# A gated attention and MLP decode step: the order of the first loads, and keys transposed ahead of the query

## The chip, the cores and the metric

The kernel runs on one core of one Trainium2 chip. The metric is the device time of one execution in microseconds (us); less is better. Each time is told as the median of the runs shown. One further execution was taken with the hardware profiler; its span, in the page, runs from the first to the last instruction of the program.

## The reference

Eight sequences each decode one token `x` of 448 numbers. Two branches are computed from it and mixed by a gate. All inputs are bf16.

```python
# A: attention over the last W = 1024 of 4096 cached positions, 16 query heads on 8 key heads, Dh = 256
q = (x @ wq).reshape(B, Sq, Hq, Dh).transpose(0, 2, 1, 3)           # wq: 448 x 4096
k = jnp.repeat(k_cache[:, :, Sk - W:, :], rep, axis=1)
v = jnp.repeat(v_cache[:, :, Sk - W:, :], rep, axis=1)
p = softmax(einsum("bhqd,bhkd->bhqk", q, k) * Dh ** -0.5)
a = einsum("bhqk,bhkd->bhqd", p, v).transpose(0, 2, 1, 3).reshape(B, Sq, Hq * Dh) @ wo
# B: layer norm and a two-layer MLP, 448 -> 1792 -> 448
b = gelu(layernorm(x) @ w1 + b1) @ w2 + b2
g = sigmoid((x * gate_w).sum(-1, keepdims=True))
out = g * a + (1 - g) * b
```

Nearly all bytes are the cache: per sequence 4 MB of keys and 4 MB of values, 64 MB in all; wq and wo are 3.5 MB each, w1 and w2 some 1.5 MB each.

## The kernel before, in words

**Loads.** A ring of four slots in SBUF, 32 KB per partition each, takes all large loads (`ring`, line 82). `add` (line 108) puts loads on a plan in the order in which they are to be used. `pump` (line 98) issues the next loads of the plan as long as no more than four slots are given out and not yet used up, and `done` (line 104) counts a slot as used up and pumps. All these loads are issued by SP, one after the other. A load into a slot that was in use waits, on SP, until the last readers of the slot are done, and whatever SP has to issue later waits behind it. The plan (lines 162 to 177) is: wq; the keys of batch 0 (k0), in two halves of 2 MB; then k1, v0, k2, v1 and so on to k7, v6; w1; v7 with w2; wo in eight pieces. `half_loader` (line 115) loads one batch in two halves by heads, `pair_loader` (line 125) in one piece, `rows_loader` (line 137) a list of matrices into one slot, one behind the other.

**wq.** Its 448 rows are 384 and 64. The first 384 lie three to a partition (`wq_m`, line 147) and are loaded as one block of 4096 columns (1 MB) and one of 8192 (2 MB). The last 64 rows are cut in half, so that they fill 128 partitions of 2048 columns (`wq_t`, line 148, 512 KB). Before, all three pieces stand in one slot, the half rows first, the others behind them from column `OWQ` on (line 156).

**The start.** `moments` (line 254) turns `x` so that it can be the stationary side of the query's matmuls (`turned`, line 227, into `xw`) and takes the mean and the variance for the layer norm; its last step is a square root on ACT. `query` (line 384) computes the query of all batches in 28 matmuls of width 512 on PE: 8 and 16 over wq's two blocks (line 390, `stationary`), 4 over the half rows (line 402, `ends`). Then ACT copies the result out (`qs`, line 412), DVE turns it (`qt`, line 415), and DVE and ACT lay it out as the stationary side of the scores (`qw`, line 428, eight copies each). `gate` (line 262) takes the gate's logits on DVE, a tanh on ACT, and a few small tables (`perm`, `pick`, `mask`); `gall` and `oall` hold the gate and its complement on all partitions.

**A batch.** `transpose_keys` (line 352) turns 1024 x 8 keys so that the head dimension lies on the partitions. The work is cut in 16 blocks, eight for each of two `kt` tiles. Block 0 (in batches 2, 4 and 6 blocks 0 and 1) is turned by DVE (line 339) and laid out by 16 copies on POOL (line 347). Each other block is four transposes on PE (line 371) into one of three PSUM tiles `ktp`, and one copy out of it on ACT (the blocks in `BY_ACT`, line 377) or DVE (line 379). Between the blocks the steps of the batch before are called, by a table from block number to steps (`between`; `steps`, line 599). `scores` (line 430) does 32 matmuls against `qw` into `S_ps`, `top` (line 447) takes the maximum. `expo`, `turn`, `scale` and `bring` make the softmax weights of the batch before, `values` (line 502) multiplies them with the values, `finish` and `spread` collect the results.

**The order of the program** is written out by hand in lines 617 to 638; each engine works through its own instructions in that order:

```python
    moments()
    query()
    gate()
    transpose_keys(0)
    scores(0)
    top(0)
    for b in range(1, NB):
        transpose_keys(b, steps(b - 1))
        scores(b)
        top(b)
        values(b - 1)
```

**The end.** After the last values the MLP's second layer and the output projection run as 46 chunks of matmuls while wo's pieces arrive, with a few filling matmuls between them (`run_on`, line 650); DVE adds two partial sums (line 690), and two stores write the result.

Of the kernel before, what the change touches and what calls it, by code (L numbers as in the profile page):

```python
# [11 lines left out]
BF16 = mybir.dt.bfloat16  # L12
# [5 lines left out]
def kernel(  # L18
# [15 lines left out]
    nc = tc.nc  # L34
    P = nc.NUM_PARTITIONS
# [3 lines left out]
    HD = A_wq.shape[1]  # L39
# [18 lines left out]
    QN = 512  # L58
# [22 lines left out]
    consts = ctx.enter_context(tc.tile_pool(name="consts", bufs=1))  # L81
# [16 lines left out]
    def pump():  # L98
        while len(slots) < min(len(plan), consumed[0] + RING):
            t = ring.tile([P, SLOT], BF16, tag="slot", name="slot")  # L100
            plan[len(slots)](t)
            slots.append(t)

    def done(n=1):
        consumed[0] += n
        pump()

    def add(key, loader):
        index[key] = len(plan)
        plan.append(loader)  # L110

    def slot(*key):
        return slots[index[key]]

    def half_loader(src, b):
        def load(t):
            for i in range(NG):
                v = src[b, i:Hkv:NG, kv_base:Sk, :].rearrange(
                    "a (s c) d -> s a (c d)", c=NCK
                )  # L120
                nc.sync.dma_start(t[:, i * HS : (i + 1) * HS], v)

        return load
# [13 lines left out]
    def rows_loader(pieces):  # L137
        def load(t):
            o = 0
            for ap in pieces:  # L140
                n = ap.shape[-1]
                nc.sync.dma_start(t[:, o : o + n], ap)
                o += n

        return load

    wq_m = A_wq[0:DM, :].rearrange("(p r) n -> p (r n)", r=NR)
    wq_t = A_wq[DM:D, :].rearrange("r (h n) -> (r h) n", h=2)
# [4 lines left out]
    OW1T = NR * F  # L153
    OW2 = OW1T + FH
    wq_r = [wq_m[:, 0:HD], wq_m[:, HD : NR * HD]]
    OWQ = HD // 2

    def last_values(t):
        pair_loader(A_v_cache, NB - 1, 2)(t)
        nc.sync.dma_start(slot("w12")[:, OW2 : OW2 + FB * D], w2_v)  # L160

    add(("wq",), rows_loader([wq_t] + wq_r))
    add(("k", 0), half_loader(A_k_cache, 0))
    for b in range(1, NB):
        add(("k", b), (half_loader if b == NB - 1 else pair_loader)(A_k_cache, b))
        add(("v", b - 1), pair_loader(A_v_cache, b - 1))
# [11 lines left out]

    x_sb = consts.tile([NB, D], BF16)
    consts.tile([P, SHIFT], F32, name="shift")  # L180
    pump()
    nc.scalar.dma_start(x_sb[:], xf)
    g_b = consts.tile([NB, D], BF16)
# [70 lines left out]
    def moments():  # L254
        turned(0, nc.vector.tensor_copy, nc.vector.tensor_copy)
        nc.vector.bn_stats(stats[:], x_sb[:])
        nc.vector.bn_aggr(mv[:], stats[:])
        nc.scalar.activation(
            rstd[:], mv[:, 1:2], ACT.Sqrt, bias=eps_t[:], scale=1.0
        )  # L260

    def gate():
        prod = consts.tile([NB, D], F32)
        gl = consts.tile([NB, 1], F32)
        nc.vector.scalar_tensor_tensor(
            prod[:],
            in0=x_sb[:],
            scalar=1.0,
            in1=g_b[:],
            op0=ALU.mult,  # L270
            op1=ALU.mult,
            accum_out=gl[:],
        )
        gth = consts.tile([NB, 1], F32)
        nc.scalar.activation(gth[:], gl[:], ACT.Tanh, scale=0.5)
        nc.vector.tensor_copy(
            perm[:].rearrange("p (s a) -> p s a", a=QD),
            ident[:].rearrange("p (a s) -> p s a", a=QD),
        )
        nc.vector.reduce_sum(  # L280
            pick[:],
            ident[:].rearrange("p (g b) -> p b g", g=QD)[:, 0:NB, :],
            axis=AXIS.X,
        )
        nc.vector.reduce_sum(
            mask[:],
            ident[:]
            .rearrange("p (s o a) -> p a o s", a=QD, o=1)
            .to_broadcast([P, QD, rep, SK]),
            axis=AXIS.X,  # L290
        )
        nc.vector.tensor_scalar(
            g32[0:NB, 0:1], gth[:], 0.5, 0.5, op0=ALU.mult, op1=ALU.add
        )
        nc.vector.tensor_scalar(om[:], gth[:], -0.5, 0.5, op0=ALU.mult, op1=ALU.add)
        gt = consts.tile([BL, BL], F32)
        nc.vector.transpose(gt[:], g32[:])
        gb = consts.tile([BL, BL], F32)
        nc.vector.stream_shuffle(gb[:], gt[:], [0] * BL)
        for i in range(QD):  # L300
            nc.scalar.copy(gall[BL * i : BL * (i + 1), :], gb[:, 0:NB])
        nc.vector.tensor_scalar(oall[:], gall[:], -1.0, 1.0, op0=ALU.mult, op1=ALU.add)
# [20 lines left out]
    def stationary(a, r):  # L323
        o = (a * NX + r) * GAP + BL
        return flat[:, o : o + NB]

    def ends(a, x2):
        o = (a * NX + NR) * GAP
        m = GAP + NB + BL * x2
        o += 0 if x2 else BL  # L330
        return flat[:, o : o + m], m
# [20 lines left out]
    def transpose_keys(b, between=None):  # L352
        between = between or {}
        kn = slot("k", b)[:].bitcast(F32)
        for hh in range(NG):
            kt = ktpool.tile([P, QD, NCK, SK, NJ], BF16, tag="kt", name="kt")
            KT[hh] = kt
            for i in range(NCK // CB):
                g = hh * (NCK // CB) + i
                n = 2 if b in DOUBLE else 1  # L360
                if g < n:
                    if g == 0:
                        turn_blocks(kn, kt, n * CB)
                    for step in between.get(g, ()):
                        step()
                    continue
                ktp = ps_kt.tile([P, CB, P, NJ], BF16, tag="ktp", name="ktp")
                words = ktp[:].bitcast(F32)
                for c in range(CB):
                    o = (hh * NCK + i * CB + c) * P  # L370
                    nc.tensor.transpose(  # L371
                        words[:, c, :, 0], kn[:, o : o + P], ident_f[:]
                    )
                dst = kt[:, :, i * CB : (i + 1) * CB, :, :]
                src = ktp[:].rearrange("p c (s a) t -> p a c s t", a=QD)
                if g in BY_ACT:
                    nc.scalar.copy(dst, src)  # L377
                else:
                    nc.vector.tensor_copy(dst, src)  # L379
                for step in between.get(g, ()):  # L380
                    step()
        done()

    def query():
        w = slot("wq")
        for r in range(NR):
            for n in range(W // QN):
                for t in range(QD):
                    o = OWQ + r * HD + t * W + n * QN
                    nc.tensor.matmul(  # L390
                        S_ps[BL * t : BL * t + NB, n * QN : (n + 1) * QN],
                        lhsT=stationary(0, r),
                        rhs=w[:, o : o + QN],
                        start=(r == 0),
                        stop=False,
                        skip_group_check=True,
                    )
        for n in range(W // QN):
            for x2 in range(2):
                lhsT, m = ends(0, x2)  # L400
                o = x2 * W + n * QN
                nc.tensor.matmul(  # L402
                    S_ps[0:m, n * QN : (n + 1) * QN],
                    lhsT=lhsT,
                    rhs=w[:, o : o + QN],
                    start=False,
                    stop=(x2 == 1),
                    skip_group_check=True,
                )
        done()  # L410
        qs = work.tile([P, W], BF16, tag="w0", name="qs")
        nc.scalar.activation(qs[:], S_ps[:], ACT.Copy, scale=qscale)  # L412
        qt = work.tile([P, 2, rep, QD, NJ, BL], BF16, tag="w2", name="qt")
        for h in range(2):
            nc.vector.transpose(  # L415
                qt[:, h].rearrange("p r i j b -> p (r i) j b"),
                qs[:, h * W // 2 : (h + 1) * W // 2].rearrange(
                    "p (m e j) -> p m j e", e=BL, j=NJ
                ),
            )  # L420
        qv = qw[:].rearrange("p j b t (u m) -> p j b t u m", u=NG)
        for i in range(QD):
            for g in range(QD):
                dst = qv[BL * i : BL * (i + 1), :, :, g, :, 0:rep]
                src = qt[BL * g : BL * (g + 1), :, :, i, :, 0:NB].rearrange(
                    "p k r j b -> p j b k r"
                )
                (nc.vector.tensor_copy, nc.scalar.copy)[g % 2](dst, src)
# [185 lines left out]
            d[14] = [norm]  # L614
        return d

    moments()
    query()
    gate()
    transpose_keys(0)  # L620
    scores(0)
    top(0)
    for b in range(1, NB):
# [19 lines left out]
    w = slot("wo")  # L643
# [17 lines left out]
    for i, (lhsT, rhs) in enumerate(wide):  # L661
# [4 lines left out]
            rhs=rhs,  # L666
# [9 lines left out]
    for i, (lhsT, rhs) in enumerate(narrow):  # L676
        k = part[i]
        for h in range(2):
# [4 lines left out]
                rhs=rhs[:, h * DO : (h + 1) * DO],  # L683
# [39 lines left out]
```

## Time and profile before

| what | value |
|---|---|
| median of the runs shown | 189.7 us (189.7, 190.16, 189.7) |
| the profiled execution's own time | 189.85 us |
| its span | 188.1 us, 2798 instructions |
| PE busy in the span | 119.9 us (64%) |
| DVE busy | 95.3 us (51%) |
| ACT busy | 90.8 us (48%) |
| POOL busy | 67.1 us (36%) |
| read from HBM | 77.69 MB, 413 GB/s over the span |
| granted TensorE clock, mean | 0.873 |

How to read it: an engine is busy when it works on an instruction; shares are of the span. No engine is busy for two thirds of the span. The loads go over 16 DMA engines; the page gives their mean busy share and what they moved, in 40 slices of 4.7 us. The chain of waits is followed back from the last instruction, at each step to what released it, so it shows one path through the execution that ends last, with the loads as steps of it. A load is issued on SP in some 0.6 us, and is then in a queue until it lands; the time from issue to landing (36.5 us in the median for keys of 4096 KB) is therefore mostly waiting in the queue. The lines that matter are shown and read in the prediction.

### The profile page before, as it was taken

The numbers are of one execution on the slowest core, as the hardware profiler recorded it, in microseconds if no ns is written. First come the engines' busy times: TensorE is split into PE (matmuls) and PEld (weight loads), VectorE is DVE, ScalarE is ACT, GpSimd is POOL, SyncE is SP. The second block draws the span as 40 slices with busy tenths as digits, with TensorE's granted clock in tenths as the row PEclk, the third lists the DMA queues.
The fourth block names the chain that finished last, engine by engine and source line by source line (L and its number), as shares of the span: only waits on it lengthen the run. The fifth ranks groups of instructions, "written<-read, shape, count | busy, mean of one in ns | idle before, by whom it ended". The sixth has DMA issues, their size and how long they took to land.

```text
span 188.1 us, 2798 instructions
## 1 busy us (share of the span) xinstructions
PE 119.9 (64%) x1103; PEld 78.7 (42%) x1104; DVE 95.3 (51%) x166; ACT 90.8 (48%) x115; POOL 67.1 (36%) x143
## 2 busy tenths in 40 slices
PE   0255078778778396890684959943968885353772
PEld 0013077476357135650663457614853662110221
DVE  7304543664287726840682228824763773762511
ACT  2003879489469426941295129820891994010000
POOL 8000075093069605800398029101991840000000
PEclk9999859969999759997599678996699999955899
DMA  6999999999999999999999999999999999999991
GB/s 219 446 422 435 432 432 425 435 428 428 432 434 425 427 428 428 439 425 428 428 439 422 439 425 432 428 435 425 432 428 435 428 428 419 417 427 441 413 396 42
DMA packets 6771, 77.85 MB, mean 414 GB/s; under 512 B 588, under 2 KB 1128, under 8 KB 1896
## 3 DMA queue, kind: packets, MB, share of 16 engines
q1 hardware_dynamic: 6712, 77.68, 97.1%
q8 instruction: 8, 0.13, 0.2%
q10 hardware_dynamic: 48, 0.02, 0.0%
q14 instruction: 3, 0.02, 0.0%
HBM read 77.69 MB, written 0.01 MB: 413 GB/s over the span
## 4 chain that ended last, share of the span: by engine, by line
DMA 77%; PE 10%; POOL 5%; DVE 3%; ACT 2%; issue 1%; SPq 0%; POOLq 0%; ACTq 0%; DVEq 0%
DMA slot<-in_A_k_cache_dram 51%; DMA slot<-in_A_v_cache_dram 12%; DMA slot<-in_A_wo_dram 9%; POOL kt L347 5%; DMA slot<-in_A_wq_dram 5%; PE ktp L371 5%; ACT kt L377 2%; DVE kt L379 1%; PE S_ps L436 1%; PE S_ps L390 1%; PE S_ps L402 1%; PE PO L507 1%; DVE EB L463 1%; DVE B L339 1%; PE S_ps L680 0%
## 5 line engine op out<-in xcount | busy, mean ns | idle before, releaser
L347 POOL COPY kt<-B 32x128 f32<-32x128 f32 (+1 forms) x128 | 62.8, 490 | 85.2 <-DVE B L339 72.0
L371 PE MATMUL ktp<-ident_f,slot 128*128 128x128 f32 x468 | 69.8, 306 | 32.5 <-DMA slot<-in_A_k_cache_dram 17.6
L377 ACT COPY kt<-ktp 128x1024 bf16<-128x1024 bf16 x77 | 72.6, 1031 | 25.3 <-PE ktp L371 25.1
L371 PEld LDWEIGHTS ktp<-ident_f,slot 128*128 128x128 f32 x468 | 59.3, 157 | 45.9 <-issue 17.9
L379 DVE COPY kt<-ktp 128x1024 bf16<-128x1024 bf16 x40 | 27.4, 685 | 17.7 <-PE ktp L371 17.5
L507 PE MATMUL PO<-slot,ET 128*16 128x512 bf16 x256 | 19.2, 447 | 7.3 <-DMA slot<-in_A_v_cache_dram 7.3
L436 PE MATMUL S_ps<-kt,qw 128*4 128x512 bf16 x256 | 18.4, 433 | 7.9 <-POOL kt L347 7.9
L454 ACT ACTIVATE E<-S_ps,nmx 128x1024 f32<-128x1024 f32 x8 | 8.9, 1115 | 24.8 <-DVE nmx L449 24.8
L449 DVE TENSOR_REDUCE nmx<-S_ps 128x1 f32<-128x1024 f32 x8 | 9.8, 1225 | 19.8 <-PE S_ps L436 19.8
L339 DVE STREAM_TRANSPOSE B<-slot 128x512 f32<-128x512 f32 (+1 forms) x8 | 7.3, 909 | 20.5 <-DMA slot<-in_A_k_cache_dram 20.5
L507 PEld LDWEIGHTS <-ET 128*16 128x16 bf16 x256 | 7.8, 101 | 17.9 <-issue 13.5
L436 PEld LDWEIGHTS <-qw 128*4 128x4 bf16 x256 | 6.2, 88 | 16.6 <-issue 11.5
L463 DVE STREAM_TRANSPOSE EB<-E 128x1056 f32<-128x1056 f32 x8 | 10.2, 1278 | 0.3
L390 PE MATMUL S_ps<-slot,xw 128*8 128x512 bf16 x24 | 2.9, 618 | 10.6 <-DMA slot<-in_A_wq_dram 10.6
L523 DVE STREAM_TRANSPOSE T<-PO 128x512 f32<-128x512 f32 x8 | 5.6, 704 | 3.7 <-PE PO L507 3.7
L490 DVE TENSOR_TENSOR ET<-sm,mask 128x512 bf16<-128x512 f32 x8 | 5.5, 692 | 3.4 <-PE sm L482 3.4
L415 DVE STREAM_TRANSPOSE qt<-qs 128x512 bf16<-128x512 bf16 x2 | 1.3, 690 | 9.9 <-ACT qs L412 9.9
L390 PEld LDWEIGHTS <-xw 128*8 128x8 bf16 x24 | 0.7, 100 | 11.9 <-issue 6.0
L412 ACT ACTIVATE qs<-S_ps 128x1024 bf16<-128x1024 f32 x1 | 1.0, 1024 | 8.5 <-PE S_ps L402 8.5
L585 ACT ACTIVATE zb<-za 128x448 f32<-128x448 f32 x1 | 0.6, 579 | 8.3 <-DVE za L584 8.3
L652 PE MATMUL warm<-slot,ident 128*128 128x512 bf16 (+1 forms) x11 | 4.0, 428 | 0.2 <-issue 0.2
L461 DVE RECIPROCAL E<-total 128x32 f32<-128x32 f32 x8 | 2.8, 344 | 1.4 <-ACT E L454 1.3
(81 smaller groups left out, 56.7 us busy)
## 6 DMA issues: line engine op xcount, KB each, us to landing
slot<-in_A_v_cache_dram SPq DMA_DIRECT2D x7, 4096.0 KB, 29.8
slot<-in_A_k_cache_dram SPq DMA_DIRECT2D x6, 4096.0 KB, 36.5
slot<-in_A_k_cache_dram SPq DMA_DIRECT2D x4, 2048.0 KB
slot<-in_A_v_cache_dram SPq DMA_DIRECT2D x2, 2048.0 KB
slot<-in_A_wq_dram SPq DMA_DIRECT2D x1, 2048.0 KB
slot<-in_A_wo_dram SPq DMA_DIRECT2D x2, 896.0 KB
slot<-in_B_w_dram SPq DMA_DIRECT2D x1, 1568.0 KB
slot<-in_B_w_dram SPq DMA_DIRECT2D x1, 1344.0 KB, 22.2
```

Source lines behind the costliest of these rows:

```text
L339: nc.vector.transpose(B[:].rearrange("p c w s a -> p (c w s a)"), kn[:, 0 : n * P],)
L347: nc.gpsimd.tensor_copy(words[BL * w : BL * (w + 1), :, 0:n, g * S8 : (g + 1) * S8, 0], B[BL * g : BL * (g + 1), :, w].rearrange("p c s a ...
L371: nc.tensor.transpose(words[:, c, :, 0], kn[:, o : o + P], ident_f[:])
L377: nc.scalar.copy(dst, src)
L379: nc.vector.tensor_copy(dst, src)
L436: nc.tensor.matmul(S_ps[BL * t : BL * t + UR, n * QN : (n + 1) * QN], lhsT=qw[:, j, b, t, rep * u : rep * u + UR], rhs=KT[u][:, t, n * CQ ...
L449: nc.vector.reduce_max(nmx[:], S_ps[:], axis=AXIS.X, negate=True)
L454: nc.scalar.activation(E[:, 0:W], S_ps[:], ACT.Exp, bias=soft.pop(b)[:], scale=1.0, accum_out=total[:],)
L463: nc.vector.transpose(EB[:].rearrange("p c r -> p (c r)"), E[:])
L490: nc.vector.tensor_tensor(ET[:].rearrange("p c u a r -> p (c u) a r"), sm[:] .rearrange("p k (o r) -> p k o r", o=1) .to_broadcast([P, NCK ...
L507: nc.tensor.matmul(PO[BL * t : BL * t + Hq], lhsT=ET[:, c].rearrange("p u a r -> p (u a r)"), rhs=vn[:, c], start=(c < QD), stop=(c >= NCK ...
L523: nc.vector.transpose(T[:, 0 : NG * n], PO[:].rearrange("p u (e j) -> p u j e", j=J8))
```

## The change

Three things change. wq's half rows get a tile of their own, `wq_b` (4 KB per partition), which is loaded first of all, from within the loader of k0. k0 then stands ahead of wq on the plan, so its slot is the ring's first and wq's two blocks come behind it, in the second slot. And in the program `transpose_keys(0)` stands first; `moments` is called from within it, after block 7, and `gate` and `query` follow behind the keys, in that order. Each call of `done` stays in its function, so the slot of k0 is now used up before that of wq: k2, the next load of the plan, waits for the readers of k0, and v1, the one after it, for the query. Line numbers after the change are four or five higher from line 163 on.

```diff
@@ -153,14 +153,18 @@
     wq_r = [wq_m[:, 0:HD], wq_m[:, HD : NR * HD]]
-    OWQ = HD // 2
+    OWQ = 0
 
     def last_values(t):
         pair_loader(A_v_cache, NB - 1, 2)(t)
         nc.sync.dma_start(slot("w12")[:, OW2 : OW2 + FB * D], w2_v)
 
-    add(("wq",), rows_loader([wq_t] + wq_r))
-    add(("k", 0), half_loader(A_k_cache, 0))
+    def first(t):
+        nc.sync.dma_start(wq_b[:], wq_t)
+        half_loader(A_k_cache, 0)(t)
+
+    add(("k", 0), first)
+    add(("wq",), rows_loader(wq_r))
     for b in range(1, NB):
@@ -178,6 +182,7 @@
     consts.tile([P, SHIFT], F32, name="shift")
+    wq_b = consts.tile([P, HD // 2], BF16)
     pump()
@@ -402,7 +407,7 @@
                     S_ps[0:m, n * QN : (n + 1) * QN],
                     lhsT=lhsT,
-                    rhs=w[:, o : o + QN],
+                    rhs=wq_b[:, o : o + QN],
                     start=False,
@@ -614,10 +619,9 @@
-    moments()
+    transpose_keys(0, {7: [moments]})
+    gate()
     query()
-    gate()
-    transpose_keys(0)
     scores(0)
     top(0)
```

## The prediction

> **What bounds the kernel now.** I read the page's second part first (how full the transfers are), then the chain of waits in order of time (what the end hangs on), then SP's own instructions in order of time (when each load is issued), then the busy time by windows.
>
> ```profile
> DMA  6999999999999999999999999999999999999991
> GB/s 219 446 422 435 432 432 425 435 428 428 432 434 425 427 428 428 439 425 428 428 439 422 439 425 432 428 435 425 432 428 435 428 428 419 417 427 441 413 396 42
> ...
> q1 hardware_dynamic: 6712, 77.68, 97.1%
> q8 instruction: 8, 0.13, 0.2%
> ```
>
> The 16 DMA engines are full from the second slice of 4.7 us to the last but one, at 417 to 446 GB/s but for the ragged ends. Nothing in the middle is a pause of the transfers. 77.68 of the 77.85 MB are this kernel's loads, which stand in one queue, SP's.
>
> ```profile
> 1.65 9.96 DMA slot<-in_A_wq_dram
> ...
> 15.42 36.52 DMA slot<-in_A_k_cache_dram
> ...
> 61.19 29.64 DMA slot<-in_A_k_cache_dram
> ...
> 100.40 29.30 DMA slot<-in_A_k_cache_dram
> ...
> 145.65 21.89 DMA slot<-in_A_v_cache_dram
> ...
> 167.56 16.77 DMA slot<-in_A_wo_dram
> ```
>
> The columns are start, length, what. The engines are met on this chain only between two loads. The ends give the pace: k2 (the keys of batch 2) lands at 15.42 + 36.52 = 51.94, k4 at 61.19 + 29.64 = 90.83, k6 at 100.40 + 29.30 = 129.70. Each step is four loads of 4096 KB (16.78 MB): 38.89 and 38.87 us, so 9.72 us a load and 431 GB/s, equal in a busy and in an idle stretch. The last load that the chain waits for lands at 167.56 + 16.77 = 184.33; PE's twelve matmuls, DVE's sum and the store fill the rest to 188.1.
>
> ```profile
> 86.00:88.00 2.00, 0.00 (x0) 0.00 (x0) 0.00 (x0) 0.00 (x0) 0.00 (x0) 0.75 0.97 410
> 88.00:90.00 2.00, 0.00 (x0) 0.00 (x0) 0.00 (x0) 0.00 (x0) 0.00 (x0) 0.50 1.00 426
> ...
> 94.00:96.00 2.00, 1.74 (x17) 1.47 (x16) 1.54 (x4) 2.00 (x4) 1.88 (x4) 1.00 1.01 434
> ```
>
> Here the columns are busy PE, PEld, DVE, ACT and POOL, then clock, DMA share, GB/s. From 86 to 90 no engine works and the loads run on: the computation has nothing left to do. So two things must hold for the time to stay: SP's queue never runs empty, and the computation has caught up before the last load. How full the queue is, SP's rows tell:
>
> ```profile
> 15.42 0.60 SPq L131 DMA_DIRECT2D slot<-in_A_k_cache_dram  x1
> 33.21 0.60 SPq L131 DMA_DIRECT2D slot<-in_A_v_cache_dram  x1
> ...
> 46.93 0.65 SPq L131 DMA_DIRECT2D slot<-in_A_k_cache_dram  x1
> 50.62 0.64 SPq L131 DMA_DIRECT2D slot<-in_A_v_cache_dram  x1
> ```
>
> These are k2, v1, k3 and v2. By 9.72 us a load from 51.94, the load ahead of each lands at 42.2 (v0), 51.9, 61.7 and 71.4. So SP issues 26.8, 18.7, 14.7 and 20.8 us before the queue would be empty. I worked out the later ones in the same way; none has less than 14.7.
>
> **The change, part by part.** *The loads.* Same count (three pieces of wq, two halves of k0, then k1 and v0), same bytes, same sizes; wq's half rows, 512 KB, are first as before. Only wq's 1024 and 2048 KB pieces go behind k0. SP's seven issues take 4.0 us as before (0.73 to 4.70). In the trace wq's pieces end the waits of PE at 6.80 and 11.65, and k0's first half at 16.52: 4.85 us for 2048 KB, 2.4 for 1024. So k0's halves land at 6.80 + 2.4 = 9.2 and 14.1, wq's pieces at 16.5 and 21.4, and k1 where it did, near 31.1. Cost: nothing, and the end of the stream does not move.
>
> *The extra tile.* 4 KB per partition; it moves the tiles behind it. No row shows that an address matters; bounds of plus and minus 0.3 us, the spread between the runs before (189.7 to 190.16) being the nearest row; I take 0.
>
> *Keys ahead of the query.* What was ready at 16.52 and was held up by ACT until 23.39 (qs 1.02, the qw copies 2.44, table load 1.28, the gate's 0.20 and 0.82) now starts at 9.2. ACT: first copy near 9.8, five copies at 1.03 to 15.0. The moments, put behind the seventh block, hold up DVE from about 13 for 0.54 + 0.98 + 0.83 + 0.69 + 0.61 + 0.17 = 3.8 us to about 17, and ACT's square root waits for them (0.29; its table is one more load of 1.28, since copies now stand ahead of it). Then five more copies to 22.5. POOL's 16 copies at 6.14 / 14 = 0.44 us run beside this, 9.9 to 17. So k0 is used up near 22, and k2, which waits for that now rather than for the query, is issued at 22 and not 15.42. Cover: 42.2 - 22 = 20 us. Upper bound: all of the old 16.52 to 33.21 counted from 9.2, plus the 3.8 and 1.28 + 0.29: 31.3, still 11 us ahead.
>
> *Query and gate behind.* PE: 1.03 + 1.88 + 1.87 = 4.8 us from 22 to 26.8 (both pieces of wq have landed). ACT has done the gate by 25.5. Then qs to 27.8, DVE's turn 1.30 to 29.1, qw's copies 2.44 to 31.6, scores 2.0 to 33.6. Before, these scores ran from 33.11 to 35.12. That is the whole gain of the computation: 1.5 us, bounds -3 (PE at the granted clock of 0.50 seen from 24 to 28 would double its 4.8) and +3. v1 is issued at 26.8 in place of 33.21; the three bias loads go behind it as before.
>
> *Where the 1.5 us go.* Batch 1's keys follow at once, as k1 has landed by 31.1. They end near 45.3 in place of 46.8, and the values of batch 0 near 49. Then PE stands until k2 lands, 51.94, as it did before (it sat idle 1.50 us there). From there on both kernels have the same work, started by the same landings. If the start came out 3 us late, not early, batch 2 would begin late, but the idle 86 to 90 takes that up, and the queue's 14.7 us of cover is not touched. Sum: 0 us on the profiled execution's 189.85 us (188.1 of span and 1.75 around it). The median of the runs shown is 0.15 lower, 189.7, which I give.
>
> **A rule against the trace.** The Trainium skill (DMA: Bandwidth & Descriptors, Where 436 GB/s comes from) puts the ceiling of these transfers at 435.2 GB/s. The trace's 431 agrees; by the page 77.68 MB take 178.5 us at the least, an estimate, so that no order of the loads could win more than some 4 us of the 182.7 that the stream took here.
>
> **The rivals.**
>
> 1. *Faster: the start was on the path after all.* If the last landing hung on when slots come free, 1.5 us earlier scores would be 1.5 us at the end: 188.2. For it: the chain passes the first scores' waits, and the first slice moves only 219 GB/s. Against it: each issue stands 14.7 us or more ahead of need. Chance 0.13.
>
> 2. *Slower: one DMA engine is held up twice.* Beside the loads run the eight packets of q8, 16 KB of instructions each. The trace's landings, engine by engine, show v0 complete on 15 engines at 40.78 and on the sixteenth at 42.27: just after the q8 packet of 36.12, so 1.5 us for one packet. Later more engines lag by as much, none by more: so far each packet has met another engine, and the end is set by an engine that was hit once. The new order moves the times at which PE's stream asks for these packets. If two meet on one engine, the last load lands 1.5 us later: 191.2. It decides from the second hit of one engine. Against it: there are as many instructions on PE as before, so as many packets, and their turn over the engines looks regular. Chance 0.17. The Trainium skill (Runtime: NRT & Kernel Launch, Instruction fetch mechanics) says that such 16 KiB blocks are fetched ahead, "mostly hidden". For PE the trace bears it out, for the load stream it doesn't, as the 1.5 us show; by the page this rival would cost nothing.
>
> 3. *The queue runs dry*, because k2 now waits for k0 instead of wq: each us beyond 39 at which k2 is issued (its first bytes need about 1 us, by the first load's 0.73 to 1.65) would be a us at the end. With 31.3 as the upper bound I put it inside rival 2's chance, at 0.01.
>
> **How the numbers follow.** This kernel's measurement can tell about 0.3%, 0.57 us, from no change. No change: 0.70, with a range of its own of 189.2 to 190.2 (the 0.3 us of the tile's place, and 0.2 for where in its round the late engine stands). Faster 0.13, slower 0.17. The range that holds 8 in 10 takes in the likeliest case and the slower one: 189.1 to 191.2; below it 0.13 are left out.
>
> **What would show it.** Right: k2 issued at 20 to 24, v1 near 27, PE's first transposes near 9.2, the first scores 0 to 3 us earlier, and PE again waiting for k2 near 52, for k4 near 90.8, for wo near 184.3. The slices of GB/s stay between 415 and 446. Wrong: a slice under 400 before the last, an issue of SP less than 5 us ahead of need, a landing of k2 off by over 0.5 us, or batch 2 begun after its keys have landed.

## The result, and the profile after

The changed kernel takes **191.44 us**, the median of 12 runs (190.19 to 192.11), against 189.8 for the kernel before, also of 12 (189.61 to 190.16). The ratio is 1.0075, with a 95% interval of 1.0051 to 1.0099: slower, by 1.4 us by the ratio, 1.6 by the two medians. Even its fastest run is slower than the slowest of before, and its runs fall into two groups: four at 190.19 to 190.37, eight at 191.41 to 192.11. The profiled execution is of the second group: 192.11 us with a span of 190.4, against 189.85 and 188.1 before, so 2.26 us longer. It is this one that the following lines dissect. Every ratio here and below is over the runs within 1.5% of a kernel's fastest, which leaves out two runs of the loads alone (193.07 and 194.33) and one of the rows 1 MB apart (192.85).

The page of the changed kernel, its transfers in 40 slices of the span and two of its queues:

```profile
DMA  6999999999999999999999999999999999999970
GB/s 203 403 413 430 437 437 441 427 410 434 437 430 433 418 427 434 437 434 430 413 430 441 437 427 437 417 427 441 434 430 434 423 420 424 420 436 424 419 293 17
...
q1 hardware_dynamic: 6712, 77.68, 96.2%
q8 instruction: 8, 0.13, 0.2%
```

Packets and bytes are the same as before to the last one. Two places differ: the second and third slice (403 and 413, in place of 446 and 422), and the end, where the last slice but one fell from 396 to 293. Between them the engines are as full as they were.

The chain of waits of the changed kernel (start, length, what):

```profile
1.19 10.27 DMA slot<-in_A_k_cache_dram
...
25.34 28.95 DMA slot<-in_A_k_cache_dram
...
63.55 29.56 DMA slot<-in_A_k_cache_dram
...
103.26 28.73 DMA slot<-in_A_k_cache_dram
...
149.65 20.22 DMA slot<-in_A_v_cache_dram
169.88 16.75 DMA slot<-in_A_wo_dram
```

Start and length add up to the landings. The first half of k0 lands at 11.46, 2.3 us later than the 9.2 predicted. k2 lands at 54.29, k4 at 93.11, k6 at 131.99 and the last load at 186.63: later than before by 2.35, 2.28, 2.29 and 2.30. So the loss is there after the first twelve microseconds, and the size of it stays the same to the end. The step from k2 to k4 is 38.82 us (38.89 before).

The stretches of the start, in the changed kernel (stretch, length, busy PE, PEld, DVE, ACT, POOL, clock, DMA share, GB/s):

```profile
2.00:4.00 2.00, 0.00 (x0) 0.00 (x0) 0.52 (x2) 0.95 (x1) 2.00 (x6) 1.00 0.92 342
4.00:6.00 2.00, 0.00 (x0) 0.00 (x0) 0.00 (x0) 0.00 (x0) 0.87 (x3) 1.00 0.87 328
6.00:8.00 2.00, 0.00 (x0) 0.00 (x0) 0.00 (x0) 0.00 (x0) 0.00 (x0) 1.00 0.97 385
8.00:10.00 2.00, 0.00 (x0) 0.00 (x0) 0.00 (x0) 0.00 (x0) 0.00 (x0) 1.00 1.02 434
```

and in the kernel before:

```profile
4.00:6.00 2.00, 0.00 (x0) 0.08 (x1) 1.79 (x8) 0.00 (x0) 0.97 (x3) 1.00 1.03 420
6.00:8.00 2.00, 1.03 (x8) 0.24 (x9) 0.62 (x2) 0.29 (x1) 0.00 (x0) 1.00 1.04 442
```

From 4 to 8 us, when k0's first half has taken the place of wq's blocks, 328 and 385 GB/s stand against 420 and 442. The DMA share at 4 to 6 is 0.87, though SP has issued all seven loads by 5.9 us (wq's three, k0's two, k1 and v0): packets take longer, and for part of the time some engines move none.

Which engines, the trace's landings tell: each load is done by 16 engines, each of which reports its own end. In microseconds, for the same loads in both profiled executions:

| load | before: 15 engines | before: last | after: 12 engines | after: the other four |
|---|---|---|---|---|
| k0, first half | 15.97 to 16.48 | 16.48 | 9.02 to 9.42 | 10.31, 10.88, 11.40, 11.46 |
| k1 | 30.57 to 31.05 | 31.05 | 31.01 to 31.31 | 32.21, 32.78, 33.29, 33.36 |
| v0 | 40.27 to 40.78 | 42.27 | 40.73 to 41.03 | 41.93, 42.50, 43.05, 44.62 |

Twelve engines come out of k0's first half where I had put all (9.2). Four come out 1.3 to 2.4 us later, and 22 us on they are still 1.2 to 2.35 us behind. So a late engine neither catches up here nor is relieved by another. A load counts as landed when its last engine is done, so the latest engine sets every landing, the last one too.

Packets of instructions (q8) add to this. The first starts at 36.12 before and 37.30 after, and holds its engine for 1.5 us. Before, it met an engine that was on time: lateness 0.5 became 2.0. After, it met one of those that were 2.3 late, and made it 3.89. So in both kernels one engine falls 1.5 us behind its own start, but in the changed one it started 2.3 behind. Later packets make other engines late, yet none later than this. The very last load, a small piece of wo that the chain does not name, lands engine by engine from 183.16 to 184.95 before and from 183.51 to 187.21 after. Of the 2.26 us between these ends 0.35 are lost by the first engine, too, and 1.91 are wider spread (3.70 against 1.79).

### The profile page after: what moved, and what is told of

It is laid out like the page before. It is cut to its first block, busy times and chain, and to the rows that moved or that the text cites. A ratio compares the mean times of both kernels' runs of the same rounds, so it can differ in the third digit from the quotient of the medians.

```text
span 190.4 us, 2801 instructions
## 1 busy us (share of the span) xinstructions
PE 123.0 (65%) x1104; PEld 79.7 (42%) x1104; DVE 94.7 (50%) x166; ACT 92.2 (48%) x116; POOL 66.8 (35%) x143
## 4 chain that ended last, share of the span: by engine, by line
DMA 71%; PE 13%; POOL 5%; DVE 5%; ACT 3%; issue 2%; SPq 0%; POOLq 0%; DVEq 0%
DMA slot<-in_A_k_cache_dram 51%; DMA slot<-in_A_v_cache_dram 11%; PE ktp L376 9%; DMA slot<-in_A_wo_dram 9%; POOL kt L352 5%; ACT kt L382 3%; PE PO L512 1%; DVE kt L384 1%; PE S_ps L441 1%; DVE EB L468 1%; DVE B L344 1%; PE S_ps L684 0%; DVE xw L245 0%; DVE xt L240 0%; DVE stats L261 0%
## 5 line engine op out<-in xcount | busy, mean ns | idle before, releaser
L376 PE MATMUL ktp<-ident_f,slot 128*128 128x128 f32 x468 | 71.8, 309 | 40.6 <-DMA slot<-in_A_k_cache_dram 30.7
L441 PE MATMUL S_ps<-kt,qw 128*4 128x512 bf16 x256 | 20.5, 456 | 13.0 <-POOL kt L352 7.5
L459 ACT ACTIVATE E<-S_ps,nmx 128x1024 f32<-128x1024 f32 x8 | 8.9, 1114 | 26.8 <-DVE nmx L454 26.8
L512 PE MATMUL PO<-slot,ET 128*16 128x512 bf16 x256 | 18.4, 432 | 3.0 <-DMA slot<-in_A_v_cache_dram 3.0
L441 PEld LDWEIGHTS <-qw 128*4 128x4 bf16 x256 | 7.2, 91 | 22.8 <-issue 17.4
L487 PE MATMUL sm<-EZ,perm 128*128 128x128 bf16 x8 | 1.8, 223 | 4.4 <-DVE EZ L474 4.4
L474 DVE SCALAR_TENSOR_TENSOR EZ<-EB,gall 128x128 bf16<-128x128 f32 x8 | 3.7, 458 | 0.0
L545 DVE TENSOR_TENSOR oP<-Y 32x128 bf16<-32x128 f32 x8 | 3.0, 371 | 0.3
L433 ACT COPY qw<-qt 32x64 bf16<-32x64 bf16 x8 | 2.4, 295 | 1.5 <-DVE qt L420 1.4
```

The lines of the kernel that those rows point to most:

```text
L376: nc.tensor.transpose(words[:, c, :, 0], kn[:, o : o + P], ident_f[:])
L441: nc.tensor.matmul(S_ps[BL * t : BL * t + UR, n * QN : (n + 1) * QN], lhsT=qw[:, j, b, t, rep * u : rep * u + UR], rhs=KT[u][:, t, n * CQ ...
L459: nc.scalar.activation(E[:, 0:W], S_ps[:], ACT.Exp, bias=soft.pop(b)[:], scale=1.0, accum_out=total[:],)
L512: nc.tensor.matmul(PO[BL * t : BL * t + Hq], lhsT=ET[:, c].rearrange("p u a r -> p (u a r)"), rhs=vn[:, c], start=(c < QD), stop=(c >= NCK ...
```

## The experiments

The theory was formed from these landings: *the order of the loads alone costs the time, because k0, as the first large load, sets some engines back, and an engine that is behind stays behind.* The rivals: the new order of PE's program makes two instruction packets meet on one engine (the prediction's second rival); the own tile of the half rows; or the late use of k0. Each ratio below is against the kernel before, run on the same chip beside it.

### The two halves of the change, each alone

The kernel before with only the new order of its loads (half rows in their old place):

```diff
+    def first(t):
+        half_loader(A_k_cache, 0)(t)
+        nc.sync.dma_start(slot("wq")[:, OWQ : OWQ + HD], wq_r[0])
+        nc.sync.dma_start(slot("wq")[:, OWQ + HD : OWQ + NR * HD], wq_r[1])
-    add(("wq",), rows_loader([wq_t] + wq_r))
-    add(("k", 0), half_loader(A_k_cache, 0))
+    add(("wq",), rows_loader([wq_t]))
+    add(("k", 0), first)
```

> The old program (moments, query, gate, then keys) and no tile of its own for the half rows; only the loads stand in the new order: half rows, both halves of k0, then wq's 1024 and 2048 KB. Theory A (the first key packets, met by engines that have just started, hold up a few of the 16 DMA engines by up to 2.4 us, and a late engine stays late to the end): as the changed kernel, 190.2 to 192.1 with a median near 191.4, and k0's first half landing near 11.5 in a slow execution. Theory B (the new order of PE's instructions brings two instruction packets onto one DMA engine): 189.8, as PE's order is the old one. Theory C (the moved addresses behind the new tile): 189.8.

The changed kernel, own tile and program order included, with the old order of loads:

```diff
     def first(t):
+        k0 = slot("k", 0)
         nc.sync.dma_start(wq_b[:], wq_t)
-        half_loader(A_k_cache, 0)(t)
-    add(("k", 0), first)
-    add(("wq",), rows_loader(wq_r))
+        nc.sync.dma_start(t[:, 0:HD], wq_r[0])
+        nc.sync.dma_start(t[:, HD : NR * HD], wq_r[1])
+        half_loader(A_k_cache, 0)(k0)
+    add(("k", 0), lambda t: None)
+    add(("wq",), first)
```

> The new program and the tile of its own, but the loads in the old order: half rows, wq's 1024 and 2048 KB, then k0. Theory A: 189.8, k0's first half landing at 16.5 on every engine. Theory B: 191.4, since PE's order is the new one. Theory C: 191.4, since the tile is there.

Measured: the loads alone give 192.22 us, ratio 1.0101 [1.0074, 1.0127], from 189.74 to 194.33 (11 runs). The program alone gives 189.76, ratio 1.0001 [0.9992, 1.0009], from 189.64 to 190.01 (11 runs). So the tile and PE's new order carry nothing by themselves, and the loss comes with the order of the loads. With that the prediction's second rival, as it was put there, falls: the new order of instructions by itself moves no packet to where it hurts.

The 1.0101 is not the price of the lateness alone. In the only profiled execution of the loads alone, its slowest (194.33), the latest engine leaves k0's first half 2.77 us behind the first. But there the old program waits for all of wq before it turns the keys, so that k3 is issued at 59.58 in place of 46.93, and the queue runs empty: k3 lands first 11.60 us behind v1, in place of 9.72.

```profile
58.00:60.00 2.00, 1.65 (x21) 1.12 (x24) 1.09 (x2) 1.61 (x3) 0.00 (x0) 1.00 0.86 365
60.00:62.00 2.00, 2.00 (x44) 0.93 (x40) 0.49 (x1) 0.60 (x1) 0.00 (x0) 1.00 0.68 222
```

The changed kernel has no such pause. That the order of the loads is the cause of its loss rests on this lateness, which is there without the tile and the new program, and on the following kernels, which keep both.

### One piece of wq between the half rows and the keys

The same kernel again, with wq's block of 1 MB (`wq_r[0]`) ahead of the keys and that of 2 MB (`wq_r[1]`) behind them:

```diff
     def first(t):
+        k0 = slot("k", 0)
         nc.sync.dma_start(wq_b[:], wq_t)
-        half_loader(A_k_cache, 0)(t)
+        nc.sync.dma_start(t[:, 0:HD], wq_r[0])
+        half_loader(A_k_cache, 0)(k0)
+        nc.sync.dma_start(t[:, HD : NR * HD], wq_r[1])
...
```

> The changed kernel with wq's 1024 KB block (8 KB packets) between the half rows and k0, and the 2048 KB block behind k0. Theory A: if a start of some 6 us with wq's rows is enough to get the engines going, 189.8 to 190.2, and k0's first half lands near 11.6 with all engines within 0.6 us. Theories B and C: 191.4.

The second kernel has the two blocks the other way round, 2 MB ahead of the keys and 1 MB behind them:

> The changed kernel with wq's 2048 KB block between the half rows and k0, and the 1024 KB block behind k0. Its packets are 16 KB like those of the keys, but from consecutive rows. Theory A in the form that large packets at the start are what holds engines up: 191.4, with a spread of over 1 us in the landing of that block. Theory A in the form that it is the keys' addresses (four heads, 4 MB apart, read at once): 189.8, with a spread under 0.6 us. Theories B and C: 191.4.

Measured: 189.77, ratio 0.9999 [0.999, 1.0007], with 1 MB in front, and 189.75, ratio 0.9999 [0.9991, 1.0008], with 2 MB in front (11 runs each). In the first the keys' first half lands on all engines within 0.51 us, and the last load at 184.92. The start of that kernel:

```profile
2.00:4.00 2.00, 0.00 (x0) 0.00 (x0) 0.52 (x2) 0.95 (x1) 2.00 (x5) 1.00 0.99 360
4.00:6.00 2.00, 0.00 (x0) 0.00 (x0) 0.00 (x0) 0.00 (x0) 0.88 (x3) 1.00 0.98 388
6.00:8.00 2.00, 0.00 (x0) 0.00 (x0) 0.00 (x0) 0.00 (x0) 0.00 (x0) 1.00 1.10 467
```

The share stays at 0.98 and over. These keys are the same bytes from the same addresses into the same slot, 2.4 us later, and are harmless. The second kernel also rules out that a 2 MB load with packets of 16 KB is what hurts in this place: wq's block is one, and its engines end within 0.42 us of each other. The first keeps the new program, and it is no faster than the kernel before: PE starts on the keys at 11.89 and not at 16.5, and nothing comes of it.

### What it is about the keys

A row of k0's first half is 16 KB, and the half is taken from four heads, 4 MB apart. Five kernels change one thing about that each. With one piece of 2 MB in place of four (this leaves out batch 0's own keys; the time alone counts):

```diff
-        half_loader(A_k_cache, 0)(t)
+        for i in range(NG):
+            v = A_k_cache[0, i, :, :].rearrange("(p c) d -> p (c d)", c=NCK)
+            nc.sync.dma_start(t[:, i * HS : (i + 1) * HS], v)
```

> The changed kernel, but each half of batch 0's keys is replaced by the 2 MB of one head's cache, which stand in one piece in HBM (so batch 0 works on wrong keys; bytes, packets and loads are the same). If the lateness comes from the addresses of the key loads (rows of four heads, 4 MB apart, for each DMA engine), then it goes: 189.8, and the first half lands near 9.2 with all engines within 0.6 us. If any 16 KB packets that come out of the cache first, or the mere lack of wq's rows in front, are enough: 190.2 to 192, a landing after 10 us, as in the changed kernel.

Measured: 189.74, ratio 0.9998 [0.999, 1.0007] (11 runs), spread 0.71 in the first half, last landing 184.89. The right keys with each half in two loads with packets of 8 KB (columns cut in half):

```diff
-        half_loader(A_k_cache, 0)(t)
...
+            h = HS // 2
+            for k in range(2):
+                nc.sync.dma_start(t[:, i * HS + k * h : i * HS + (k + 1) * h],
+                                  v[:, :, k * h : (k + 1) * h])
```

> The changed kernel with each half of batch 0's keys loaded in two loads of 1 MB, 8 KB packets in place of 16 KB, with the same four heads in each. If the size of the first packets is the cause: 189.8 to 190.0. If it is the addresses: 190.2 to 192.

Measured: 190.83, ratio 1.0087 [1.0058, 1.0115] (9 runs, 190.38 to 192.4); the profiled execution, one of the faster ones at 190.6, has a spread of 0.99 when the first half is complete. So neither the place in the queue alone nor the packet's size: rows in one piece are harmless in the very place where rows from four heads are not, and these hurt with packets of either size.

The stretches show it side by side. The kernel with the keys in one piece:

```profile
4.00:6.00 2.00, 0.00 (x0) 0.00 (x0) 0.00 (x0) 0.00 (x0) 0.87 (x3) 1.00 0.99 389
6.00:8.00 2.00, 0.00 (x0) 0.00 (x0) 0.00 (x0) 0.00 (x0) 0.00 (x0) 1.00 1.05 451
```

Is it that the four places lie a power of two apart? The Trainium skill (DMA: Bandwidth & Descriptors, Latency and other measured facts) has copies whose rows lie 4 MiB apart at 103 GB/s, and at 214 with 4 KiB added to the pitch; it calls the cause an inference. Two kernels (again without batch 0's own keys) tested it here: four places 4 MB and 4 KB apart, and four places 1 MB apart (2048 in place of 8200).

```diff
-        half_loader(A_k_cache, 0)(t)
+        rows = A_k_cache.rearrange("b h s d -> (b h s) d")
+        for i in range(NG):
+            o = i * Sk
+            v = rows[o : o + QD * 8200, :].rearrange("(a q) d -> a q d", a=QD)
+            v = v[:, 0:W, :].rearrange("a (s c) d -> s a (c d)", c=NCK)
+            nc.sync.dma_start(t[:, i * HS : (i + 1) * HS], v)
```

> The changed kernel, batch 0's keys taken from four places 4 MB + 4 KB apart in place of the four heads 4 MB apart (batch 0 works on wrong keys; bytes, packets and loads are the same). If the distance of just 4 MB, a power of two, is what sets some engines back at the start: 189.8, the first half on all engines by 9.7. If any rows that lie far apart do it: 190.2 to 192.

> The changed kernel, batch 0's keys taken from four places 1 MB apart (batch 0 works on wrong keys). If a power of two of this size is enough: 190.2 to 192. If it needs the heads' 4 MB, or places further apart than 1 MB: 189.8.

Measured: 191.89, ratio 1.0106 [1.0088, 1.0124] (6 runs), with the 4 KB, and 190.65, ratio 1.0055 [1.0034, 1.0075] (8 runs), at 1 MB apart. The kernel with the 4 KB, at its start:

```profile
4.00:6.00 2.00, 0.00 (x0) 0.00 (x0) 0.00 (x0) 0.00 (x0) 0.87 (x3) 1.00 0.82 311
6.00:8.00 2.00, 0.00 (x0) 0.00 (x0) 0.00 (x0) 0.00 (x0) 0.00 (x0) 1.00 1.09 385
```

Four engines are late by 1.6, 1.8, 2.5 and 2.5 us: the picture of the changed kernel again. So the pitch's power of two is not it. By the Trainium skill's rule the 4 KB should have restored the rate; here they did not, and the same halves with their pitch of 4 MB run at some 431 GB/s in the kernel before, as k0 from 11.6 to 16.48 us and as k7. The copies that the Trainium skill tells of run between two places in HBM and not into SBUF; no run here shows those, and the rule doesn't explain this start.

k0 as one load of 4 MB over all eight heads, 2 MB apart, as batches 1 to 6 are loaded:

```diff
-        half_loader(A_k_cache, 0)(t)
+        pair_loader(A_k_cache, 0)(t)
```

> The changed kernel with batch 0's keys in one load, as the other batches have them: each engine reads rows of eight heads, 2 MB apart, in place of two times four heads 4 MB apart. Same keys, same result. If the distances between heads are the cause, it is late as well: 190.2 to 192. If only the halves' 4 MB do it: 189.8.

Measured: 191.74, ratio 1.0091 [1.0075, 1.0107] (6 runs); the load lands from 13.86 to 15.94 on its engines. The shape that is harmless from k1 to k6 hurts in the first place.

### What it is about the start

The keys even ahead of the half rows:

```diff
-        nc.sync.dma_start(wq_b[:], wq_t)
         half_loader(A_k_cache, 0)(t)
+        nc.sync.dma_start(wq_b[:], wq_t)
```

> The changed kernel with wq's half rows behind batch 0's keys: the keys are the very first load. If the start of the engines on keys is the cause, the half rows (512 KB, landed at 4.2) were no help: 191 or more, as many engines late as in the changed kernel or more. If it needs the change from 4 KB packets to 16 KB ones, 189.8.

Measured: 190.31, ratio 1.0027 [1.0016, 1.0037] (7 runs, 190.08 to 190.38), milder than expected. Of the 16 engines' first packets ten take 1.0 to 1.2 us in place of the usual 0.61 and six take 0.61 to 0.73, yet the first half ends within 0.67 us (7.88 to 8.56). The whole stream is some 0.35 us late, and no engine is far behind the others. So, in this execution and by the small spread of the times, keys from four heads as the very first load do not set single engines back. They do in the place behind the half rows.

If it were a matter of touching far-apart rows for the first time, small loads of the same rows (64 bytes of each) ahead of everything should cure it:

```diff
+    touch = consts.tile([P, NG, 32], BF16)
+    for i in range(NG):
+        nc.scalar.dma_start(touch[:, i, :], A_k_cache[0, i:Hkv:NG, kv_base:Sk, :].rearrange(
+            "a (s c) d -> s a (c d)", c=NCK)[:, :, 0:32])
     pump()
```

> The changed kernel with two small loads more at the head of ACT's queue, which read the first 64 bytes of each of the 256 rows of batch 0's keys into a tile that nothing uses. If what sets engines back is the first touch of rows that lie far apart (as opposed to the burst of large reads from them at the start), the small loads pay for it and the first half of the keys lands on all engines within 0.6 us: 189.8 to 190.1. If it is the burst: 190.2 to 192, and a spread of 1 us or more in that landing.

Measured: 193.4, ratio 1.0191 [1.0168, 1.0214] (6 runs). The keys' first half lands with a spread of 1.31 us (9.30 to 10.62), as expected if it is the burst. The time lies beyond both forecasts and is no clean test: the second small load lands only at 10.3 to 11.5 us and holds up what ACT issues behind it, x and the gate's weights among them, and the whole stream runs slower to the end (9.79 us a load in place of 9.73, some 1 us in all), for a reason that no run shows. A cleaner answer stands in other kernels: in the kernel before, in those with wq ahead and in the next one k0's rows are touched for the first time, too, only later, and no engine is set apart.

If it were that the queue starts from empty, a queue that runs empty later should show the same. Here all of wq comes first, and a small load into k0's slot makes k0 wait for wq to be done; the second kernel has the keys in one piece behind the same pause (without batch 0's own keys):

```diff
     def first(t):
+        k0 = slot("k", 0)
         nc.sync.dma_start(wq_b[:], wq_t)
-        half_loader(A_k_cache, 0)(t)
+        nc.sync.dma_start(t[:, 0:HD], wq_r[0])
+        nc.sync.dma_start(t[:, HD : NR * HD], wq_r[1])
+        nc.sync.dma_start(k0[:, 0:32], A_wq[0:P, 0:32])
+        half_loader(A_k_cache, 0)(k0)
...
```

> The changed kernel with all of wq in front of batch 0's keys, and a small load of wq behind it into the keys' slot, so that the keys' first load waits on SP until wq has landed and the queue stands empty for some 2 us. If a start from an empty queue on rows that lie far apart sets engines back, the first half of the keys (due near 19) lands with a spread of over 1 us, and the time is 2 us of pause plus 1 to 2 us, 192.5 to 194. If it is a matter of the first microseconds of the execution: a spread of under 0.6 us, and the pause alone, 191.3 to 192.

> As the run before it, but the keys of batch 0 are replaced by the cache of one head per half, rows in one piece (batch 0 works on wrong keys). Both theories: a spread of under 0.7 us and the pause alone, 191.3 to 192.

Measured: 192.96, ratio 1.0169 [1.014, 1.0199], with the rows of four heads, and 192.94, ratio 1.0168 [1.0139, 1.0198], with the rows in one piece (2 runs each). Both lose the pause, and lose it alike. By its time the first came out as forecast for engines set apart, 192.5 or more, but only since the pause cost more than forecast; the landings and the second kernel decide. The first of the two, around its pause:

```profile
12.00:14.00 2.00, 0.00 (x0) 0.00 (x0) 0.00 (x0) 0.00 (x0) 0.00 (x0) 1.00 0.51 131
14.00:16.00 2.00, 0.00 (x0) 0.00 (x0) 0.00 (x0) 0.00 (x0) 0.00 (x0) 1.00 0.97 393
```

Behind it the keys' first half lands within 0.54 us on all engines (0.79 in one piece). So a queue that runs empty at 12 us sets no engine apart, and keys from four heads behind it are as harmless as keys in one piece. With the two kernels above that have a block of wq in front, this ties the effect to the first microseconds of the execution.

### The changed kernel once more

> The changed kernel once more, on the same chip as the three above: 190.2 to 192.1, median near 191.4. By the landings of k0's first half, the time should follow the latest engine: about 189.8 plus the latest engine's lateness beyond 0.5 us, plus up to 1.5 us where the first packet of PE's instructions (near 37 us) meets that engine.

Measured: 191.87, ratio 1.0108 [1.0083, 1.0134] (6 runs, 190.65 to 192.86). Its profiled execution is its fastest, 190.65 us. In it the latest engine leaves k0's first half only 1.12 us behind the first; the first instruction packet meets an engine that was nearly on time (v0: lateness 1.58, not 3.89); the engines end from 183.41 to 185.77. The profiled executions side by side (lateness is that of the last engine behind the first, in us):

| kernel | lateness, k0's first half | lateness, v0 | lateness, last load | last load landed | time | time less landing |
|---|---|---|---|---|---|---|
| before | 0.51 | 2.00 | 1.79 | 184.95 | 189.85 | 4.90 |
| 1 MB of wq ahead | 0.51 | 1.54 | 1.69 | 184.92 | 189.76 | 4.84 |
| keys in one piece | 0.71 | 1.82 | 1.64 | 184.89 | 189.73 | 4.84 |
| packets of 8 KB | 0.99 | 1.61 | 2.26 | 185.61 | 190.60 | 4.99 |
| changed, again | 1.12 | 1.58 | 2.36 | 185.77 | 190.65 | 4.88 |
| one load, eight heads (all of k0) | 2.08 | 2.03 | 3.35 | 186.82 | 191.73 | 4.91 |
| changed | 2.44 | 3.89 | 3.70 | 187.21 | 192.11 | 4.90 |
| 4 MB and 4 KB apart | 2.50 | 3.96 | 3.83 | 187.56 | 192.45 | 4.89 |

The time is the latest engine's end plus 4.8 to 5.0 us, in all of them. And the lateness at the end is that of k0's first half plus 0.9 to 1.3 us, in harmful and harmless kernels alike. So the packets of instructions come on top everywhere, and what tells the kernels apart is the lateness with which the engines leave k0's first half. The second execution of the changed kernel is no exception: its late engines are hit as well, only later, and behind the packet of 149 us the lateness is 2.45. It is faster than the first by 1.46 us, and 1.32 of these stand already at k0's first half, 1.12 in place of 2.44. Whether the two groups of the changed kernel's runs, with middles at 190.3 and 191.7, differ in this way is not shown: the other runs have no profile.

**What is shown and what stays open.** Shown: the loss comes with the order of the loads, not with the tile or the program; it is gone when 1 or 2 MB of wq stand ahead of the keys, and gone when the keys come in one piece; it sets four of 16 engines back by 1.3 to 2.4 us in the changed kernel's profiled execution; an engine's lateness stays to the end; and the end follows the latest engine. How late the engines come out differs from one execution to the next (2.44 and 1.12 in the two profiled). Open: why loads from far-apart rows set single engines back only in the first microseconds, and there in the place behind the half rows, but not as the very first load. A power of two between the rows, the packet's size, the first touch of these rows and a queue that starts from empty have been ruled out as the whole reason, the last by two runs of each kernel and one profile. What else runs in the first microseconds (x's load, the memsets on POOL and DVE) was not varied on its own.

## Why the prediction was wrong, by its own steps

- **The bound** was right: the load stream sets the time, at 431 GB/s and 38.8 us for four loads, also after. What it lacked: the stream is 16 streams, and the end is that of the latest one. I read their common rate and not their spread, though I had used single landings for the second rival. The cover of 14.7 us or more does not hold for the last two pieces of wo: they are issued at 172.46 and 176.19, and the pieces ahead of them land at 184.33 and 184.64, so 11.9 and 8.5 us, which was enough.
- **"Cost: nothing, and the end of the stream does not move"** is the step that failed. I gave each piece its duration from its old place in the queue (4.85 us for a half of k0). Twelve engines kept to it (9.02 to 9.42 for the 9.2 predicted), four did not, and k2 came at 54.29 in place of 51.94. Same bytes and same sizes were not the same transfer in the first place behind the half rows. Moving the keys there cost 2.3 us in the profiled execution and 1.4 by the ratio of the runs.
- **The extra tile** at 0 was right: with the old loads, tile and new program together give 1.0001.
- **The keys ahead of the query.** SP's rows of the changed kernel, k2, v1, k3, v2:

```profile
25.34 0.60 SPq L131 DMA_DIRECT2D slot<-in_A_k_cache_dram  x1
27.05 0.60 SPq L131 DMA_DIRECT2D slot<-in_A_v_cache_dram  x1
...
48.64 0.65 SPq L131 DMA_DIRECT2D slot<-in_A_k_cache_dram  x1
52.30 0.64 SPq L131 DMA_DIRECT2D slot<-in_A_v_cache_dram  x1
```

  k2's issue was put at 22, or 31.3 at most, and 20 to 24 was the sign of being right; it came at 25.34. Of the 3.3 us the late keys make 2.3, and 1.1 is work on them, 13.9 us from their landing in place of 12.8. v1 was put at 26.8 and came at 27.05, by luck: the query began 3.2 us late, but v1 waits for its 24 matmuls over wq's two blocks only, and these took 1.76 us where I had counted 4.8 for all 28. The cover was read rightly: the load ahead of k2 (v0) lands at 44.62, that ahead of k3 (v1) by 9.72 us a load near 64.0, so these two are issued 19 and 15 us ahead of need.

- **Query and scores.** PE's rows of the changed kernel (start, busy, what, and in brackets the idle time before it and what ended that):

```profile
11.59 4.88 PE L376 MATMUL ktp<-ident_f,slot 128*128 128x128 f32 x24 [11.59 <-DMA slot<-in_A_k_cache_dram]
...
33.52 4.46 PE L441 MATMUL S_ps<-kt,qw 128*4 128x512 bf16 x32 [5.53 <-DVE qw L433]
...
54.43 1.50 PE L376 MATMUL ktp<-ident_f,slot 128*128 128x128 f32 x12 [2.18 <-DMA slot<-in_A_k_cache_dram]
```

  The first scores began at 33.52, against 31.6 forecast and 33.11 before, so the gain of 1.5 us did not come; and they ran 4.46 us in place of 2.01, since PE's granted clock was 0.50 from 33 to 38 (before, it was 1.00 from 33 to 36). The bound of -3 covers that. As forecast it made no difference: PE then stands idle for k2 (2.18 us before 54.43), and even with harmless loads this program gives 189.77.
- **Rival 1** (faster) did not occur: k0's scores were never on the path. **Rival 3** (the queue runs dry) did not either; only with the old program behind the new loads it did, at 60 us.
- **Rival 2** (one engine held up twice) had the right shape: the end is late because one engine was held up twice, and its 191.2 lies 0.24 below the median. That nearness is luck: the first holdup is not a packet of instructions but the keys' start, and the reason that I gave, a new order of PE's instructions, costs nothing alone. The second holdup is one: the packet at 37.30 took an engine from 2.3 late to 3.89, as v0's landing shows. The Trainium skill's "mostly hidden" (Runtime: NRT & Kernel Launch, Instruction fetch mechanics) fails for the load stream here, too.
- **The range** ended at that rival's 191.2, that is, at one hit more than before. I had no term for a transfer that runs unlike its former self in a new place, though "a slice under 400" stood among the signs, nor for a kernel whose own runs spread over 1.9 us (before: 0.55). The sign that named it was the landing of k2 off by over 0.5 us; the second and third slice, at 403 and 413, only grazed theirs.

## What to carry to other kernels

Here a stream of loads over 16 DMA engines was 16 streams, and an engine that fell behind stayed behind as long as the queue was full: look at the landings engine by engine, and ask of each edit what it does to the latest one, not to the mean rate. When loads are reordered in the first microseconds, a duration from another place in the queue is no price for the new one, and a megabyte of wq, whose pieces of 8 KB lie only 24 KB apart, ahead of keys from far apart was worth 1.4 us here. Where the end hangs on the loads alone, computing earlier brings nothing, as the same program behind harmless loads shows (0.9999).

## What the runs showed of the hardware that was not expected

- One packet of 16 KB takes 611 ns, the median before and after. A load of 4096 KB is 16 such packets on each engine and takes 9.72 us, so one packet follows the other after some 607 ns: 16,384 bytes by 607 ns are 27.0 GB/s, and sixteen of them 431.9. While the queue was full, no late engine caught up in any trace here.
- In the changed kernel single packets of keys between 4 and 6 us took up to 1420 and 1609 ns; in the kernel before, the longest 16 KB packet of the first 26 us took 706. A slow packet alone is not the mark, though: with the keys in one piece behind the pause, packets took up to 1845, and the engines still came out within 0.79 us.
- A packet of instructions shows as 0.88 to 0.97 us in its queue, but the engine's loads come out 1.45 to 1.6 us later. There are eight in an execution, so up to eight engines are late at the end by one packet each.
- To let the queue run empty once, at 12 us, cost some 3.2 us (192.96 against 189.73), more than the 1.5 to 2.3 that I had expected.
